# Two block orders in a Strassen kernel on Trainium2: block 2 of A11 B11 behind block 5, and k^T v one place sooner

## The chip, the cores and the metric

The kernel runs on one core of one Trainium2 chip. The metric is the device time of one execution in microseconds (us). Times of separate runs are given as a median; one further execution was taken with the hardware profiler, and everything that is said of single instructions comes from that one.

The engines of the core are named as in the profile: PE is TensorE (PEld its weight loads), DVE is VectorE, ACT is ScalarE, POOL is GpSimd and SP is SyncE, which issues most of the loads. Each engine works through its own instructions in the order in which the program issued them.

## The reference

```python
def _attn_ref(q, k, v, g_norm):                       # (8, 8, 576, 64) each
    kv = np.einsum('bhsd,bhse->bhde', k, v)
    out = np.einsum('bhsd,bhde->bhse', q, kv)
    rms = np.sqrt(np.mean(out * out, axis=-1, keepdims=True) + 1e-06)
    return (out / rms * g_norm).astype(np.float32)
...
def _moe_ref(x, w_in, w_out, s, b):                   # x: (4608, 512), d_ff = 2048
    h = x @ w_in
    r = np.maximum(h, 0.0)
    g = s * (r * r) + b
    return (g @ w_out).astype(np.float32)
```

The output of the linear attention, with its heads laid side by side, is the x of the second part. All is float32. The two large products, x by w_in and g by w_out, are nearly all of the arithmetic.

## The kernel before, in words

**Tiling.** The 4608 rows are worked in nine units of 512 rows, u = 0 to 8. "The seventh unit" is u = 6. In each unit a first stage makes g from x and w_in, and a second stage makes the output from g and w_out. While a unit runs, the attention of the next unit is made beside it, in steps that are put between the unit's own steps.

**Strassen products.** Both stages use the Winograd form of Strassen's scheme: a product of two matrices that are cut in 2 x 2 becomes seven products of blocks, numbered 1 to 7, with sums of blocks before and sums of results after. From u = 2 on, the scheme is used on two levels: each of the seven outer products of the second stage is itself made from seven inner blocks. The outer product 1 is A11 B11, where A11 is a quarter of g and B11 a quarter of w_out. Its inner blocks are what the first part of the change reorders. The other outer products are made in the groups (2, 5), (6), (7, 3) and (4).

**Inner blocks and banks.** The function `at_two_levels` returns four functions for one group. `sums` makes sums of quarters of g on VectorE (line 256 and line 253 of the profile). `go(m)` issues the matmuls of inner block m: for A11 B11 these are four matmuls of 128 x 128, which the profile records as eight. `out_of(m)` takes the result out of PSUM, and `do` calls both. The blocks 1, 6, 5 and 3 add up in one bank named x; block 2 has a bank z; the blocks 7 and 4 share a bank y. So between two blocks in x, the value that stands there has to be copied out:

- after block 1 the copy is r1 (VectorE, line 1077), wanted for the output of block 2;
- after block 6 it is r2 (VectorE, line 1077), wanted for block 4;
- after block 5 it is r4 (for A11 B11 on ScalarE, line 1077), wanted to finish the output of block 5 with y;
- after block 3 it is an output itself (ScalarE for A11 B11, line 1077).

The output adds of the blocks 2, 5 and 4 are on VectorE (line 253). The function `keep` in `at_two_levels` makes the tiles r; each tag has one buffer, and a new writer waits for the readers of the one before.

**The second stage, `rest()`.** Its order is written out by hand. At its start it still finishes blocks of the first stage (`p3_5`, `p3_34`, and `s1`, two adds on VectorE that also need two activations of ScalarE), between the inner blocks of A11 B11.

**The ring.** From u = 2 on the pieces of w_out come through a ring of 14 slots in SBUF. `ORDER` lists the pieces (outer product, inner block) in the order in which they are wanted, `pump()` issues the next loads on SP as slots come free, and `used()` says that a piece has been read. Slots come free in the order of the list alone.

**k^T v.** For u = 1 to 6, `kv_product` makes k^T v of one further batch: 144 matmuls of 64 x 64, each with a weight load, and four copies of the results (ScalarE, line 388) into `bd_kv`. Its inputs are the first eight pieces in the ring of its unit. From u = 3 on it takes the banks z and y. Where it stands is set in `sides`, in a table `first` from a place in the first stage to what is called there. In `run` of `mm1_deep`, place 2 lies between the first x1 and the second, and place 4 between the first x6 and the first y7. `A["product"]` is the attention product of the next unit's first half, 32 matmuls of 64 x 32.

Of the kernel before, what the change touches and what calls it, by code (L numbers as in the profile page):

```python
# [10 lines left out]
FP32 = mybir.dt.float32  # L11
# [6 lines left out]
def kernel(  # L18
# [40 lines left out]
    P = 128  # L59
# [192 lines left out]
    def add(o, a, b):  # L252
        nc.vector.tensor_tensor(out=o, in0=a, in1=b, op=ALU.add)  # L253
# [136 lines left out]
    late, xT = {}, {}  # L390
# [596 lines left out]

    ORDER = [(1, 1), (2, 1), (5, 1)] + [(1, m) for m in (6, 2, 7, 5, 3, 4)]  # L990
    ORDER += [(i, m) for m in (2, 6, 7, 5) for i in (2, 5)] + [(6, 1)]
    ORDER += [(i, m) for m in (3, 4) for i in (2, 5)]
    ORDER += [(6, m) for m in (2, 6, 7, 5)] + [(7, 1), (3, 1), (6, 3), (6, 4)]
    ORDER += [(i, m) for m in (2, 6, 7, 5) for i in (7, 3)] + [(4, 1), (7, 3), (3, 3), (7, 4)]
    ORDER += [(4, m) for m in (2, 6, 7, 5)] + [(3, 4), (4, 3), (4, 4)]

# [4 lines left out]
    for u in range(1, U):  # L1001
# [4 lines left out]
        else:  # L1006
            queue_w2 += [(u, key, m) for key in DEEP for m in (6, 5)]
            queue_w2 += [(u, i, m) for i, m in ORDER]
    next_at = [0]
# [44 lines left out]
    def mm2(u, step=None, side={}):  # L1054
# [43 lines left out]
        def at_two_levels(group, other, to):  # L1098

            n = len(group)
            a = {i: {} for i in group}
            t, r = {}, {}
            cols = [slice(q * P, q * P + P) for q in range(2)]

            def quarter(i, j, h):
                g = g_pair[G_OF[i], h].rearrange("p s b t -> p (s b) t")  # L1110
                return g[:, :, j * P : j * P + P]

            def sums(which, *of):
                for i in of or group:
                    x11, x12, x21, x22 = (quarter(i, j, h) for j in range(2) for h in range(2))
                    a[i].update({2: x12, 4: x22})
                    for m in which:
                        a[i][m] = late["sub"].tile(
                            [P, FC // 4, P], FP32, name="sub",
                            tag="sub7" if m == 7 else "sub", bufs=2 if m == 7 else 6,  # L1120
                        )
                        if m == 5:
                            add(a[i][5], x21, x22)
                        elif m == 6:
                            sub(a[i][6], a[i][5], x11)
                        elif m == 7:
                            sub(a[i][7], x11, x21)
                        else:
                            sub(a[i][3], x12, a[i][6])

            def go(m, *of):
                name = {2: "z", 7: "y", 4: "y"}.get(m, "x")
                first = m in (1, 2, 7)
                if first:
                    ps = bank_of((name, group), name, 1 if name == "z" else 2)
                    t[name] = ps.rearrange("p b (m c) -> p (b m) c", c=P)[:, :n]
                for i in of or group:
                    k = group.index(i)
                    x = quarter(i, 0, 0) if m == 1 else a[i][m]
                    w = ring[u, i, m]  # L1140
                    for f in range(FC // 4):
                        matmul(
                            t[name][:, k], x[:, f], w[:, f],
                            first and k == 0 and f == 0, f == FC // 4 - 1,
                        )
                    used((u, i, m))

            def keep(name, j, q):
                if name == "r2":
                    r[name] = late["tmp"].tile([P, n, P], FP32, name="r", tag=f"r2_{n}")  # L1150
                else:
                    r[name] = late["tmp"].tile([P, 2, P], FP32, name="r", tag="r14")[:, :n]
                plus_of(
                    r[name], t["x"], other(j, cols[q]),
                    nc.scalar.copy if name == "r4" else nc.vector.tensor_copy,
                )

            def out_of(m, k=slice(0, n)):
                if m == 1:
                    keep("r1", 0, 0)  # L1160
                elif m == 2:
                    add(to(0, cols[0]), t["z"], r["r1"])
                elif m == 6:
                    keep("r2", 1, 0)
                elif m == 5:
                    keep("r4", 1, 1)
                    add(to(1, cols[1]), t["y"], r["r4"])
                elif m == 3:
                    plus_of(to(0, cols[1]), t["x"], other(0, cols[1]))
                elif m == 4:  # L1170
                    add(to(1, cols[0])[:, k], t["y"][:, k], r["r2"][:, k])

            def do(*ms):
                for m in ms:
                    go(m)
                    out_of(m)

            return sums, go, out_of, do
# [139 lines left out]
        def start_5():  # L1318
# [4 lines left out]
        sums_1, go_1, out_1, do_1 = at_two_levels(  # L1323
            (1,), lambda j, q: None, one(lambda j, q: slot(j, 1)[:, q])
        )
# [28 lines left out]
        def rest():  # L1354
            do_1(1)
            start_5()
            step["p3_5"]()
            sums_1((5, 6))
            go_25(1)
            step["p3_34"]()  # L1360
            do_1(6)
            do_1(2)
            sums_1((3,))
            go_1(7)
            step["s1"]()
            do_1(5)
            sums_25((5, 6), 2)
            sums_25((7,), 5)
            at(0)
            out_25(1)  # L1370
            do_1(3)
            sums_25((5, 6), 5)
            do_1(4)
            do_25(2)
            at(1)
            step["s3"]()
            s2((0,))
            do_25(6)
            s2((1,))
            sums_25((3,))  # L1380
            go_25(7)
            s2((2,))
            do_25(5)
            s2((3,))
            sums_6(())
            do_6(1)
            sums_6((5, 6))
            at(2)
            do_25(3)
            sums_6((7, 3))  # L1390
            do_25(4)
            if end:
                for j in range(2):
                    store("o1", j, 4 * u + j, left, queues)
            s4((0,))
            do_6(2, 6)
            s4((1, 2, 3))
            go_6(7)
            do_6(5)
            sums_73((5, 6), 7)  # L1400
            sums_73((), 3)
            go_73(1)
            with_5(0, cols[0])
            out_73(1)
            do_6(3)
            with_5(0, cols[1])
            sums_73((5, 6), 3)
            do_6(4)
            with_5(1)
            do_73(2)  # L1410
            sums_73((7,))
            at(3)
            do_73(6)
            sums_73((3,))
            at("sums")
            go_73(7)
            do_73(5)
            sums_4((5, 6))
            do_4(1)
            at(4)  # L1420
            do_73(3)
            with_7(0)
            sums_4((7, 3))
            go_73(4, 7)
            out_73(4, slice(0, 1))
            with_7(1)
            if end:
                for j in range(2):
                    store("o2", j, 4 * u + 2 + j, right, queues)
                store("o1", 0, 4 * u, right, queues)  # L1430
            else:
                store("o1", 0, 4 * u, queues=queues)
            do_4(2, 6)
            go_4(7)
            do_4(5)
            at(5)
            go_73(4, 3)
            out_73(4, slice(1, 2))
            if end:
                store("o1", 1, 4 * u + 1, right, queues)  # L1440
            else:
                store("o1", 1, 4 * u + 1, queues=queues)
            do_4(3)
            at(6)
            if end:
                store("o2", 0, 4 * u + 2, left, queues)
            else:
                store("o2", 0, 4 * u + 2, queues=queues)
            do_4(4)
            if end:  # L1450
                store("o2", 1, 4 * u + 3, left, queues)
            else:
                store("o2", 1, 4 * u + 3, queues=queues)
# [63 lines left out]
    turn, take, product, square, root, norm, turn_x = zip(*(attention(c) for c in range(4)))  # L1517
# [154 lines left out]
    def sides(u, A, B):  # L1672
# [4 lines left out]
        kv = []  # L1677
# [36 lines left out]
            }  # L1714
        else:
            first = {
                2: [A["turn"]],
                4: [A["product"], *kv],
                5: [A["back"]],
                6: [A["square"], B["turn"]],  # L1720
                7: [A["row_sum"]],
# [13 lines left out]
    for u in range(U):  # L1735
        A, B = pairs_of(u + 1) if u + 1 < U else (None, None)
# [98 lines left out]
```

## Time and profile before

| | us |
|---|---|
| median of 3 runs | 911.13 |
| lowest and highest of them | 909.51, 912.71 |
| the profiled execution's own time | 908.79 |
| its span, first to last instruction | 907.0 |
| TensorE busy | 893.4 (98%) |
| VectorE busy | 659.3 (73%) |
| ScalarE busy | 347.8 (38%) |
| GpSimd busy | 266.5 (29%) |

The busy shares are averages over the whole span. A timeline row gives the start in us from the span's start, the time that the row covers in us, the engine, the line, the operation, the tiles (out<-in), the shape and the count; in square brackets stands the idle time of the engine before it, and what ended it. A line of the waits gives the waiting engine and line, what it waited for, the total in us, how often, and the longest. Ends of matmuls are modelled, so the distance from start to start is the better measure of what a block costs on TensorE.

### The profile page before, as it was taken

What the parts mean: (1) busy time and instruction counts of PE and PEld (TensorE: products, weight loads), DVE (VectorE), ACT (ScalarE), POOL (GpSimd) and SP (SyncE); (2) the same over time, 40 slices, a digit from 0 to 9 for tenths busy, and PEclk for the clock granted to TensorE, in tenths of its full rate; (3) what the DMA queues carried; (4) which work ended last, traced back from release to release, by engine and by line L of the source; (5) the groups of instructions that cost most, each with busy time, mean ns of one, the idle gap of its engine ahead of it and who ended that gap; (6) DMA issues with size and microseconds to landing.
All of it is one profiled execution on the core that took longest, in us unless ns stands there. A gap on an engine that the chain in (4) does not pass through costs nothing.

```text
span 907.0 us, 19461 instructions
## 1 busy us (share of the span) xinstructions
PE 893.4 (98%) x7578; PEld 823.0 (91%) x7578; DVE 659.3 (73%) x1240; ACT 347.8 (38%) x584; POOL 266.5 (29%) x501
## 2 busy tenths in 40 slices
PE   7999999999999999999999999999999999999998
PEld 6888888888889998999899988998899989999998
DVE  2899686687557975798578866885779667972696
ACT  3887024521157016620463037501670066104610
POOL 2027067024732434702372027403440300021000
PEclk9999999999999999999999999999999999999999
DMA  9697947259944995389537972698349811992286
GB/s 267 218 325 215 300 111 240 59 146 396 333 121 109 301 302 139 81 289 316 163 78 229 304 242 66 166 304 271 91 95 319 276 41 52 301 292 60 56 279 186
DMA packets 118987, 184.55 MB, mean 203 GB/s; under 512 B 25200, under 2 KB 42992, under 8 KB 118896
## 3 DMA queue, kind: packets, MB, share of 16 engines
q1 hardware_dynamic: 98288, 155.36, 54.5%
q0 software_dynamic: 17152, 25.72, 9.8%
q10 hardware_dynamic: 3456, 2.23, 1.0%
q8 instruction: 60, 0.98, 0.5%
q14 instruction: 31, 0.25, 0.1%
HBM read 157.03 MB, written 26.21 MB: 202 GB/s over the span
## 4 chain that ended last, share of the span: by engine, by line
PE 93%; DVE 4%; DMA 1%; ACT 1%; issue 1%; SPq 0%; DVEq 0%
PE x_ps L92 46%; PE y_ps L92 28%; PE z_ps L92 10%; PE sx_ps L92 6%; PE y_ps L540 2%; DMA kv_sb<-in_v_dram 1%; PE kv_ps L372 1%; PE z_ps L372 1%; DVE xn L573 0%; DVE a L256 0%; DVE sub L256 0%; PE y_ps L372 0%; DVE o L253 0%; DVE xT L584 0%; DVE xs L256 0%
## 5 line engine op out<-in xcount | busy, mean ns | idle before, releaser
L1610 POOL DMA_DIRECT2D q_sb<-in_q_dram x312 | 176.2, 573 | 133.0 <-ACT a L898 77.2
L92 PE MATMUL x_ps<-w_sb,sub 128*128 128x128 f32 x1176 | 149.5, 276 | 3.1 <-ACT r L1077 2.5
L1197 POOL DMA_DIRECT2D out_dram<-o x120 | 59.6, 503 | 310.2 <-issue 152.7
L92 PEld LDWEIGHTS x_ps<-w_sb,sub 128*128 128x128 f32 x1176 | 139.7, 192 | 4.8 <-ACT r L1077 3.8
L639 ACT ACTIVATE a<-a,b_col,s_col 128x512 f32<-128x512 f32 x144 | 117.0, 813 | 27.0 <-DVE a L642 18.3
L92 PE MATMUL x_ps<-xs,ws 128*128 128x256 f32 x528 | 125.2, 380 | 0.1
L92 PE MATMUL y_ps<-xs,wb 128*128 128x256 f32 x528 | 124.6, 381 | 0.0
L92 PEld LDWEIGHTS y_ps<-xs,wb 128*128 128x128 f32 x528 | 97.1, 190 | 12.4 <-issue 0.6
L92 PEld LDWEIGHTS x_ps<-xs,ws 128*128 128x128 f32 x528 | 96.3, 190 | 11.7 <-ACT r L713 0.5
L814 ACT COPY a<-x_ps 128x512 f32<-128x512 f32 x28 | 16.4, 584 | 220.4 <-PE x_ps L92 220.4
L253 DVE TENSOR_TENSOR r<-sx_ps,a 128x256 f32<-128x256 f32 x84 | 35.4, 421 | 80.3 <-PE sx_ps L92 80.3
L92 PE MATMUL x_ps<-xT,wa 128*128 128x256 f32 x360 | 83.7, 381 | 0.1
L898 ACT ACTIVATE a<-a 128x512 f32<-128x512 f32 x112 | 69.8, 623 | 18.4 <-DVE a L260 18.4
L92 PEld LDWEIGHTS x_ps<-xT,wa 128*128 128x128 f32 x360 | 66.8, 190 | 10.4 <-issue 1.5
L92 PE MATMUL x_ps<-w_sb,a 128*128 128x128 f32 (+1 forms) x432 | 64.9, 298 | 0.0
L92 PE MATMUL y_ps<-w_sb,a 128*128 128x128 f32 (+1 forms) x416 | 62.1, 295 | 0.0
L92 PEld LDWEIGHTS x_ps<-w_sb,a 128*128 128x128 f32 x432 | 58.4, 192 | 2.9 <-issue 0.4
L92 PEld LDWEIGHTS y_ps<-w_sb,a 128*128 128x128 f32 x416 | 56.1, 192 | 2.1
L253 DVE TENSOR_TENSOR r<-x_ps,o 128x256 f32<-128x256 f32 (+1 forms) x84 | 29.6, 353 | 28.8 <-PE x_ps L92 28.1
L92 PE MATMUL y_ps<-w_sb,sub 128*128 128x128 f32 x392 | 49.5, 275 | 0.0
L256 DVE TENSOR_TENSOR a<-a,a 128x512 f32<-128x512 f32 x72 | 46.8, 684 | 0.4
L92 PE MATMUL z_ps<-w_sb,a 128*128 128x128 f32 (+1 forms) x352 | 46.9, 280 | 0.0
(184 smaller groups left out, 1452.2 us busy)
## 6 DMA issues: line engine op xcount, KB each, us to landing
w_sb<-w SPq DMA_DIRECT2D x399, 256.0 KB, 4.8
w_raw<-in_moe_w_in_dram SPq DMA_DIRECT2D x8, 1024.0 KB, 6.8
w_raw<-in_moe_w_out_dram SPq DMA_DIRECT2D x8, 1024.0 KB, 5.2
w_sb<-w SPq DMA_DIRECT2D x14, 512.0 KB, 8.7
w<-sub POOLq DMA_DIRECT2D x28, 256.0 KB, 6.1
out_dram<-o POOLq DMA_DIRECT2D x112, 64.0 KB, 3.9
w_sb<-in_k_dram SPq DMA_DIRECT2D x24, 288.0 KB, 4.7
w_sb<-in_v_dram SPq DMA_DIRECT2D x24, 288.0 KB, 4.8
```

The costliest lines, as they stand in the source:

```text
L92: nc.tensor.matmul(o, lhsT=lhsT, rhs=rhs, start=start, stop=stop, skip_group_check=True)
L253: nc.vector.tensor_tensor(out=o, in0=a, in1=b, op=ALU.add)
L256: nc.vector.tensor_tensor(out=o, in0=a, in1=b, op=ALU.subtract)
L372: nc.tensor.matmul(ps[r][(r ^ l) * HB : (r ^ l) * HB + HB, i, :], lhsT=kv[l][0][rows, j, :], rhs=kv[l][1][rows, j, :], start=(j == 0), sto ...
L540: nc.tensor.matmul(ps[l][32 * p : 32 * p + 32, r, lo:hi], lhsT=bd_kv[b % 2][rows, p, at : at + 32], rhs=st["qT"][rows, p, lo:hi], start=Tr ...
L639: nc.scalar.activation(t, t, AF.Identity, scale=s_col, bias=b_col)
L814: nc.scalar.copy(g_tile("a11", s), st["x", s])
L898: nc.scalar.square(ga[name, s], ga[name, s])
L1197: queues[s % 2].dma_start(out=view[b, jj, :, cols], in_=st[name, j][s * w : s * w + w, cols])
L1610: load()
```

## The change

In every unit from u = 2 on, inner block 2 of A11 B11 is issued behind block 5 instead of behind block 6: the order 1, 6, 2, 7, 5, 3, 4 becomes 1, 6, 7, 5, 2, 3, 4. The ring's list is changed alike. Since r1 is now still wanted when r4 is written, r4 takes another buffer, of a tag (`q4`) that the first stage uses already. The new buffer applies to r4 of all groups.

In u = 6 alone, k^T v is called at place 2 of the first stage instead of place 4, behind `A["turn"]`. Its slots of the ring come free there too. Nothing is added to or taken from what is computed.

```diff
-    ORDER = [(1, 1), (2, 1), (5, 1)] + [(1, m) for m in (6, 2, 7, 5, 3, 4)]
+    ORDER = [(1, 1), (2, 1), (5, 1)] + [(1, m) for m in (6, 7, 5, 2, 3, 4)]
...
-                    r[name] = late["tmp"].tile([P, 2, P], FP32, name="r", tag="r14")[:, :n]
+                    r[name] = late["tmp"].tile(
+                        [P, 2, P], FP32, name="r", tag="r14" if name == "r1" else "q4"
+                    )[:, :n]
...
             do_1(6)
-            do_1(2)
             sums_1((3,))
             go_1(7)
             step["s1"]()
             do_1(5)
+            do_1(2)
             sums_25((5, 6), 2)
...
             first = {
-                2: [A["turn"]],
-                4: [A["product"], *kv],
+                2: [A["turn"], *(kv if u == 6 else [])],
+                4: [A["product"], *(kv if u != 6 else [])],
```

## The prediction

> **What bounds the kernel now.** I read the page's busy table and chain first, then who waited for whom on TensorE, then the timeline around the two edits.
>
> ```profile
> PE 893.4 (98%) x7578; PEld 823.0 (91%) x7578; DVE 659.3 (73%) x1240; ACT 347.8 (38%) x584; POOL 266.5 (29%) x501
> PE 93%; DVE 4%; DMA 1%; ACT 1%; issue 1%; SPq 0%; DVEq 0%
> ```
>
> TensorE is busy 98% of the span and carries 93% of the chain that ended last; its clock is at nine tenths or more in every slice. So an edit pays if it closes a hole in TensorE's stream and costs if it opens one. The holes, from the waits of TensorE (us in total, times, longest):
>
> ```profile
> PE x_ps L92 <- ACT r L1077: 2.5, 7, 0.4
> ...
> PE z_ps L372 <- issue: 0.9, 1, 0.9
> ...
> PE x_ps L92 <- DVE r L253: 0.6, 2, 0.4
> ```
>
> The first is one hole in each of the seven units u = 2 to 8. The second is in the k^T v product of u = 6. The third lies in u = 2. Around the first, in u = 6, TensorE's timeline and then ScalarE's:
>
> ```profile
> 676.25 1.06 PE L92 MATMUL x_ps<-w_sb,sub 128*128 128x128 f32 x8
> 677.14 1.06 PE L92 MATMUL z_ps<-w_sb,a 128*128 128x128 f32 x8
> 678.03 1.06 PE L92 MATMUL y_ps<-w_sb,sub 128*128 128x128 f32 x8
> 678.93 1.06 PE L92 MATMUL x_ps<-w_sb,sub 128*128 128x128 f32 x8
> 680.34 1.16 PE L92 MATMUL x_ps<-w_sb,sub 128*128 128x128 f32 x8 [0.35 <-ACT r L1077]
> 681.33 0.83 PE L92 MATMUL y_ps<-w_sb,a 128*128 128x128 f32 x6
> ```
> ```profile
> 678.49 0.81 ACT L639 ACTIVATE a<-a,b_col,s_col 128x512 f32<-128x512 f32 x1
> 680.02 0.27 ACT L1077 COPY r<-x_ps 128x128 f32<-128x128 f32 x1 [0.72 <-PE x_ps L92]
> ```
>
> These six rows are the blocks 6, 2, 7, 5, 3, 4 of A11 B11. Four of them (6, 5, 3 and the earlier 1) grow one sum in one x bank, and each value of it is copied out before the next block adds to it. Block 5 is followed at once by block 3, so block 3 waits until ScalarE has copied r4. Undisturbed blocks start 0.893 us apart; 678.93 to 681.33 is 2.40 us for two, so the hole is 2.40 - 1.79 = **0.62 us** (0.52 of waiting, and 0.10 because the first weight load no longer runs ahead). Seven times it is 4.3 us, more than the 2.5 that the wait table counts, since modelled matmul ends overlap the next start.
>
> The k^T v hole, in the chain:
>
> ```profile
> 629.83 0.91 issue
> 630.73 0.27 PE z_ps L372
> ```
>
> It is in the middle of the product, after every tensor it needs was in use, so it waits for no data. The same product in u = 5 runs from 531.41 to the next block at 533.69, 2.28 us; here from 627.63 to 631.11, 3.48 us. The hole costs **1.20 us**. The DMA view of 628 to 629 us shows what coincides:
>
> ```profile
> q8 instruction: 1, 0.02, 5.8%
> ```
>
> **What the Trainium skill says.** "Runtime: NRT & Kernel Launch", Instruction fetch mechanics: instructions stream in blocks of 16 KiB, 256 instructions, fetched by DMA as the sequencer runs, and the cost is mostly hidden because issue is slower than the refill. The trace agrees on size (queue q8: 60 packets, 0.98 MB) but not on hiding: k^T v is 288 instructions in some 2.2 us, 7.6 ns each, and directly before it u = 6 issues 64 more for the attention product. "TensorE: Matmul & The Clock Gate", Step-by-step: weight loads are pulled ahead of running matmuls; here they start 0.11 us ahead (678.82 against 678.93), and in the hole load and matmul start together, which is the 0.10 above. "Perfetto Trace Analysis", Matmuls: independent groups should rotate through different PSUM banks so that evacuation of one hides behind the next; the z block (2) is the one that can be put between two x blocks, and y is already between 2 and 5.
>
> **Part 1: block 2 moves behind block 5 (and r4 gets another buffer), u = 2 to 8.** Same instructions, other order: 6, 7, 5, 2, 3, 4.
>
> Gap 5 to 3 now holds block 2. From 6 at 676.25: 7 at 677.14, 5 at 678.03, 2 at 678.93, 3 due at 679.82. Block 5 can be read 1.09 us after its start (678.93 to 680.02 before), so at 679.12; ScalarE is in the activation that starts at 678.49, and by the spacing of its predecessors (0.72) takes the copy at 679.21 to 679.30, ending at 679.48 to 679.57; with the 0.05 from copy to TensorE, 679.53 to 679.62. Block 3's weight load is due at 679.71. It fits with 0.1 to 0.2 us: the 0.62 goes.
>
> Gap 6 to 5 loses block 2 and keeps block 7. Block 5 needs VectorE's r2 copy of block 6, in the trace 677.34 to 677.63 after 0.47 us of idle; usable at 677.68, weight load due at 677.92. Slack 0.24: no new wait, priced at nothing by VectorE's idle time.
>
> What stands behind on VectorE: the later add of block 2 (0.21) moves behind two adds "s" and the add of block 5. Working it row by row (0.60 per 512-wide operation, 0.71 where it needs the one before): r2 at 677.34, the sum for block 3 at 677.55, s at 678.15, the second s only at 679.34, as it needs ScalarE's activation that ends at 679.30, the two output adds at 679.94 and 680.15, the next sums at 680.36. Before they began at 680.53, so VectorE leads by 0.17 us while TensorE leads by 0.62. The next demands of the group (2, 5): its second sum 6 usable at 684.07, due 684.17; r2 at 686.74, due 686.86; r4 at 689.48, due 689.54. All fit, by 0.06 to 0.12; by 691 VectorE has caught up (it idles 0.31 before 689.57 and 0.56 before 695.83 today). Full value for u = 3 to 8: 6 x 0.62 = **3.7 us**.
>
> In u = 2 those demands are late already: VectorE runs without a pause from 293 to 311 us and TensorE waits for r at 300.54 and 310.14 (the third wait above). There only VectorE's lead counts: **0.2 us**.
>
> The ring order ORDER changes alike, so weights still arrive in the order of use; 7 and 5 are wanted 0.89 us sooner, by loads issued 14 slots ahead. TensorE waits for none of these loads now; cost nothing, at most one landing (longest 10.4 us against some 12 of lead). The new buffer's r4 waits only for readers of the unit's earlier q4, long done; block 1's r1 lives 1.8 us longer, and its next writer is in VectorE's own order behind it.
>
> **Part 2: k^T v before the second x1 in u = 6.** Moved: 288 TensorE instructions, four ScalarE copies of 0.26, and eight SP loads that wait for its slots (628.8 to 632 becomes some 624.5 to 628; behind them SP holds only later loads of the same ring). No POOL issue is passed. Data: the last k or v load landed at 620.07, the product would start at 622.3: 2.2 us of slack. Banks: z and y were last read by 619.9; z is next wanted at some 627, its copies done by 625.2; ScalarE is idle then (1.14 before 624.09).
>
> Instructions: what moves behind it (second x1 16, two small blocks 16, x6 16, attention product 64) is 112 instructions. Today's stop comes at about instruction 264 of the product; that boundary would then be 88 behind its end, 1.7 us of x1, 0.9 of small blocks, 1.7 of x6 and part of the attention product later, while the fetch took some 2.4 us from packet to resumption (628.35 to 630.73). So the 1.20 goes. Against it, two fast runs now lie apart: each change of form costs a restart, 0.17 in (0.09 + 0.08) where joint entry cost nothing and 0.40 out of the attention product where 0.38 stood, +0.19. Net **1.0 us**. Bounds: from +0.2 (the hole stays or reappears) to -1.3.
>
> **Sum.** 3.7 + 0.2 + 1.0 = 4.9 us. Against the profiled execution's own 908.79 us (span 907.0 and 1.8 around it) that is 903.9; that execution is 2.3 below the median 911.13, and from the median it is **906.2**.
>
> **Rivals.** (a) VectorE becomes the bound in all units as in u = 2: slacks of 0.06 to 0.12 are as small as my row arithmetic is sure. Then TensorE keeps only VectorE's 0.17 per unit: 7 x 0.17 + 1.0 = 2.2, 908.9. For: the u = 2 waits. Against: idle rows in the other units. (b) The k^T v hole is not the fetch, or turns up at another fast stretch: 3.9 - 0.2 = 3.7, 907.4. For: other fetches pass beside k^T v without a hole; against: nothing else lies in the gap. (c) The wait only changes places: block 5 waits for r2. It decides from 0.24 us of lateness; if the copy fell behind the sum and both s (1.9 us), each unit would lose 1.9 - 0.24 + 0.10 = 1.8, 12.3 in all against 5.3 gained: 918. Against: VectorE is idle ahead of that copy in every unit. (d) The edit does nothing, if order were set elsewhere: 911.1. Against: instructions go out in program order.
>
> **Chances.** Forecast 0.62, (a) 0.17, (b) 0.14, (c) 0.04, (d) 0.03. A measurement of this kernel tells 0.3%, 2.7 us, from no change. Forecast and (b) are faster, (a) lies about the line: 0.83 faster, 0.12 same, 0.05 slower. Range 904.2 to 909.2: from the forecast less 2 (the shown runs spread 3.2) to (a).
>
> **What would show it.** TensorE's wait on r L1077 gone in all seven units, blocks 0.89 apart through 6, 7, 5, 2, 3, 4; no wait of x_ps on DVE r in u = 3 to 8; the r waits of u = 2 still there and no longer offset by the first hole; k^T v of u = 6 in 2.3 us without "issue". Wrong would be: x_ps waits on DVE r at blocks 5, or an issue hole elsewhere.

## The result and the profile after

The median fell from 911.15 us to 906.44 us (lowest 905.75, highest 907.35); the ratio is 0.9947, with a 95% interval of 0.9931 to 0.9963. The forecast was 906.2.

The profiled execution after took 906.96 us, with a span of 905.2. Against the profiled execution before, the span is only 1.8 us shorter, while the medians are 4.7 apart. So the two profiles have to be laid over each other before a cause is read from them. I took TensorE's matmuls in the order of issue, both profiles having 7578 records, and followed by how much each starts later or earlier after than before:

| where | change of the distance, us |
|---|---|
| up to 73.5 us, ahead of anything that was edited | +2.92 |
| u = 2, block 3 of A11 B11 | -0.61 |
| u = 2, 7.7 us behind it, block 5 of the group (2, 5) | +0.45 |
| u = 3, 4 and 5, block 3 of A11 B11 | -0.61, -0.61, -0.62 |
| u = 4, k^T v, nothing edited there | +0.14 |
| u = 6, k^T v and its surroundings | -1.01 |
| u = 6, 7 and 8, block 3 of A11 B11 | -0.62, -0.62, -0.62 |

Without the first row the sum is -4.7 us. The row of k^T v of u = 4 was not forecast: the product took 2.42 us in place of 2.27 in this one execution, and why is not known. The first row is the start of the program, which differs from execution to execution: in the eight profiles whose start no edit touches (those of before and after, and six of the experiments) the k^T v of u = 1 begins between 151.34 and 154.27 us. The waits of TensorE after show it in two lines (waiting engine and line, releaser, us in total, times, longest), and the third wait is what is left of u = 2:

```profile
PE kv_ps L372 <- DMA kv_sb<-in_v_dram: 2.5, 4, 1.1
PE x_ps L92 <- ACT r L713: 1.7, 2, 1.1
...
PE x_ps L92 <- DVE r L253: 1.1, 2, 0.7
```

The wait on r L1077 and the "issue" wait of z_ps are not in that list any more. The two waits on line 713 end at 71.8 and 76.1 us, in the first unit, where nothing was edited; the list of before has none. From here on "from u = 1 on" is the distance from the first k^T v matmul of u = 1 to the end of the span. It leaves the start out: 907.02 - 151.34 = 755.68 us before, 905.18 - 154.27 = 750.91 after, **4.77 us less**.

The blocks of A11 B11 in u = 6, TensorE's timeline after:

```profile
676.29 1.06 PE L92 MATMUL x_ps<-w_sb,sub 128*128 128x128 f32 x8
677.18 1.06 PE L92 MATMUL y_ps<-w_sb,sub 128*128 128x128 f32 x8
678.07 1.06 PE L92 MATMUL x_ps<-w_sb,sub 128*128 128x128 f32 x8
678.97 1.06 PE L92 MATMUL z_ps<-w_sb,a 128*128 128x128 f32 x8
679.86 1.06 PE L92 MATMUL x_ps<-w_sb,sub 128*128 128x128 f32 x8
680.75 1.06 PE L92 MATMUL y_ps<-w_sb,a 128*128 128x128 f32 x8
```

Six blocks, 0.89 apart throughout; the z row now stands between the second and third x row. ScalarE's timeline for r4, and VectorE's for r2, the two adds "s" and what follows:

```profile
678.53 0.82 ACT L639 ACTIVATE a<-a,b_col,s_col 128x512 f32<-128x512 f32 x1
679.25 0.24 ACT L1077 COPY r<-x_ps 128x128 f32<-128x128 f32 x1
```
```profile
677.38 0.29 DVE L1077 COPY r<-x_ps 128x128 f32<-128x128 f32 x1 [0.47 <-PE x_ps L92]
...
679.38 0.69 DVE L253 TENSOR_TENSOR s<-a,a 128x512 f32<-128x512 f32 x1 [0.51 <-ACT a L639]
679.99 0.28 DVE L253 TENSOR_TENSOR o<-y_ps,r 128x128 f32<-128x128 f32 x1
680.19 0.28 DVE L253 TENSOR_TENSOR o<-z_ps,r 128x128 f32<-128x128 f32 x1
680.39 0.68 DVE L253 TENSOR_TENSOR sub<-a,a 128x512 f32<-128x512 f32 x1
```

r4 is copied 679.25 to 679.49 and block 3 starts at 679.86: the copy has left the path. The wait in square brackets at 679.38 is new and falls on VectorE; its next sums start at 680.39, 0.53 after block 3, where before they started 0.19 after it (680.53 against 680.34):

```profile
680.53 0.68 DVE L253 TENSOR_TENSOR sub<-a,a 128x512 f32<-128x512 f32 x1
```

That is how much nearer to the path VectorE has come.

Inside the k^T v of u = 6 no two matmuls start more than 0.09 us apart; before, one distance was 1.12. The chain of waits behind its last matmul has no "issue" piece either (start, us, what):

```profile
625.65 1.93 PE x_ps L92 x8
627.58 0.44 PE sx_ps L92 x4
628.02 0.45 PE z_ps L92 x4
628.47 1.73 PE x_ps L92 x8
630.19 1.02 PE y_ps L540 x32
```

k^T v itself takes 2.27 us (from 623.31 to the start of the next block at 625.58), and the attention product follows behind four other blocks.

### The profile page after: what moved, and what is told of

Same layout as the page of the kernel before. It is cut to its first block, busy times and chain, and to the rows that moved or that the text cites. A ratio compares the mean times of both kernels' runs of the same rounds, so it can differ in the third digit from the quotient of the medians.

```text
span 905.2 us, 19434 instructions
## 1 busy us (share of the span) xinstructions
PE 891.9 (99%) x7578; PEld 821.9 (91%) x7578; DVE 658.7 (73%) x1240; ACT 347.6 (38%) x584; POOL 266.8 (29%) x501
## 4 chain that ended last, share of the span: by engine, by line
PE 88%; DVE 6%; DMA 3%; ACT 2%; issue 1%; DVEq 0%; ACTq 0%
PE x_ps L92 43%; PE y_ps L92 25%; PE z_ps L92 10%; PE sx_ps L92 6%; PE y_ps L540 2%; DMA w_raw<-in_moe_w_in_dram 1%; DMA kv_sb<-in_v_dram 1%; DMA w_raw<-in_moe_w_out_dram 1%; PE kv_ps L372 1%; PE z_ps L372 1%; DMA q_sb<-in_q_dram 1%; DVE xs L256 1%; DVE a L256 0%; ACT w_raw L233 0%; DVE xn L573 0%
## 5 line engine op out<-in xcount | busy, mean ns | idle before, releaser
L253 DVE TENSOR_TENSOR r<-sx_ps,a 128x256 f32<-128x256 f32 x84 | 35.4, 422 | 80.1 <-PE sx_ps L92 80.1
L253 DVE TENSOR_TENSOR r<-x_ps,o 128x256 f32<-128x256 f32 (+1 forms) x84 | 29.7, 353 | 26.7 <-PE x_ps L92 26.0
```

## The experiments

**The two edits one at a time.** The first kernel is the change with the rows of k^T v put back:

```diff
-                2: [A["turn"], *(kv if u == 6 else [])],
-                4: [A["product"], *(kv if u != 6 else [])],
+                2: [A["turn"]],
+                4: [A["product"], *kv],
```

> Block 2 behind block 5 in all units, k^T v of u = 6 where it was. My theory (two separate edits that add up): no wait of TensorE on r L1077, 0.62 us saved in each of u = 3 to 8 and 0.17 in u = 2, and the hole in the k^T v of u = 6 still there with 1.1 to 1.2 us; 3.9 us less than before from u = 1 on, some 3.7 less than the median. Rival (VectorE bounds all units): 1.2 us less. Rival (the order of blocks also moved the hole): no hole, 5 us less.

Measured: 907.37 us median against 911.59 (ratio 0.9946, 0.9932 to 0.9961); from u = 1 on 751.87, which is 3.81 less than before. The waits of TensorE still have the hole of k^T v, and nothing on r L1077:

```profile
PE z_ps L372 <- issue: 0.9, 1, 0.9
```

The second kernel is the kernel before with only the move of k^T v.

> Only k^T v of u = 6 moved, blocks in the old order. My theory: the hole of 1.2 us gone, 0.2 us of restarts added, seven waits on r L1077 as before; 1.0 us less than before from u = 1 on, which the spread of whole runs can hardly show. Rival (the hole stays with the product wherever it stands): 0.2 us more.

Measured: 910.74 us median against 911.59 (ratio 0.9987, 0.9979 to 0.9996); from u = 1 on 754.73, 0.95 less. The seven waits on r L1077 are as before, and z_ps no longer waits. 3.81 + 0.95 = 4.76, and the whole change gave 4.77: the two edits add up, and both sizes are as forecast (3.9 and 1.0).

**Is it block 2, or any block?** Here block 7 is the one put between 5 and 3; no other buffer is needed, since r1 is used up before r4 is written. k^T v stays where it was.

```diff
-    ORDER = [(1, 1), (2, 1), (5, 1)] + [(1, m) for m in (6, 2, 7, 5, 3, 4)]
+    ORDER = [(1, 1), (2, 1), (5, 1)] + [(1, m) for m in (6, 2, 5, 7, 3, 4)]
...
-            go_1(7)
+            go_1(5)
             step["s1"]()
-            do_1(5)
+            go_1(7)
+            out_1(5)
```

> Blocks of A11 B11 in the order 1, 6, 2, 5, 7, 3, 4, no new buffer, k^T v where it was: block 7 and not block 2 stands between 5 and 3. My theory (any independent block hides the copy): the same gain as with block 2, 3.9 us from u = 1 on, no wait on r L1077. Rival (it matters that block 2's add comes later on VectorE, or the new buffer): the gain differs by over 1 us or the wait on r L1077 stays.

Measured: 906.85 us median (ratio 0.9942, 0.9925 to 0.9959); from u = 1 on 752.98, only 2.70 less than before, so by the letter of the expectation the number missed by over 1 us. The place-by-place comparison says why. The wait on r L1077 is gone in all seven units, and TensorE's blocks are 0.89 apart through 5, 7 and 3 (in u = 3 they start at 389.73, 390.62 and 391.51). But in u = 2, ahead of any inner block of A11 B11, TensorE waited 0.45 us for VectorE, which had stood behind a late load of q (VectorE's timeline, this kernel):

```profile
260.64 1.25 DVE L528 STREAM_TRANSPOSE qT<-q_sb 128x1024 f32<-128x1024 f32 x1 [4.98 <-DMA q_sb<-in_q_dram]
261.81 0.65 DVE L260 CUSTOM_DVE_ANT_0 a<-y_ps,a 128x512 f32<-128x512 f32 x1
```

and the hole in the k^T v of u = 6 was 1.5 us, 0.3 longer than before. Another 0.1 is in u = 2: VectorE begins the sums of the next group 0.1 later against block 3 than with block 2, and there VectorE is the bound. Each of u = 3 to 8 loses a further 0.04, some 10 us behind block 3. Without these four losses (0.45, 0.3, 0.1 and 0.2) the gain would be some 3.75, near the other order's 3.81; the first two stand in places that the edit does not touch. The medians of whole runs, which do not hang on one execution, do not show this kernel behind: 4.7 us less than before, against 4.2 with block 2, and their intervals overlap. The theory that any independent block hides the copy stands; the new buffer and the later add of block 2 are not what pays.

**Putting the hole into its other place.** The change, with block 5 directly behind block 6:

```diff
-    ORDER = [(1, 1), (2, 1), (5, 1)] + [(1, m) for m in (6, 7, 5, 2, 3, 4)]
+    ORDER = [(1, 1), (2, 1), (5, 1)] + [(1, m) for m in (6, 5, 7, 2, 3, 4)]
...
-            go_1(7)
+            go_1(5)
             step["s1"]()
-            do_1(5)
+            go_1(7)
+            out_1(5)
             do_1(2)
```

> The change, but with block 5 directly behind block 6 (1, 6, 5, 7, 2, 3, 4). My theory: the hole comes back in its other place, in front of block 5, which waits for VectorE's r2 copy, 0.5 to 0.65 us in each of seven units; 4 us more than the change. Theory of the wait that only moves: as well, but then the change itself should show part of this. Rival (VectorE's copy is early enough by itself): no hole, time of the change.

Measured: 910.48 us median (ratio to before 0.9988, 0.9982 to 0.9995); from u = 1 on 755.23, 4.32 more than the change. The waits of TensorE:

```profile
PE x_ps L92 <- DVE r L1077: 2.7, 7, 0.4
```

The same seven holes, now behind VectorE's r2 in place of ScalarE's r4, 0.55 us each and 0.10 for the first weight load, which no longer runs ahead. So the value is neither in the engine that copies nor in the number of blocks between 6 and 3, but in having at least one block in each of the two gaps, 6 to 5 and 5 to 3.

**What the hole in k^T v is.** I counted TensorE's instructions (weight loads, matmuls and its semaphore instructions) from the start. In the kernel before, the hole of u = 6 comes after 266 instructions of k^T v. Multiples of 256 counted from there fall, in u = 3 to 5, elsewhere in the product; in u = 1 and 2 they fall at 269 and 239 without a hole, and the last section comes back to that. If the hole is a wait for the next block of instructions, spare instructions at the start must move it. They were added where TensorE waits for k and v:

```diff
-    def warm(n):
+    def warm(n, more=0):
...
+        for _ in range(more):
+            matmul(ps[:HB, 0, :HB], ident[:HB, :HB], ident[:HB, :HB], True, True)
...
-                warm((18, 7)[i])
+                warm((18, 7)[i], (16, 0)[i])
```

> The change, with 64 more TensorE instructions at the start (16 spare 64 x 64 matmuls and their weight loads, the result unused), in the first microseconds where TensorE waits for k and v. My theory (the hole is the wait for a block of 256 instructions, when a block ends late in k^T v and the attention product stands right before it): the blocks then end where they did in u = 6 before, but in u = 5, so a hole of 1.1 us with no visible cause appears in the k^T v of u = 5, and none in the other units. Rival (the hole belongs to u = 6, by its data or banks): no hole anywhere.

Measured, one execution: from u = 1 on 753.62, 2.71 more than the change. The chain of waits of this kernel, in u = 5 (start, us, what):

```profile
536.70 0.05 PE z_ps L374
536.76 1.50 issue
538.26 0.21 PE z_ps L374
```

k^T v of u = 5 took 4.07 us in place of 2.28, a hole of 1.79 where the change has none, and the k^T v of no other unit has one. The place is right; the size is 1.6 times what was expected. The rest of the 2.71 is a late load of q in u = 2 (0.4), a stop of 0.2 right behind the k^T v of u = 6, and 0.5 behind the last matmul. The start of the program has a hole of this kind too, 1.0 us in the first k^T v, which "from u = 1 on" leaves out and no expectation named.

> As the one before with 128 more instructions (32 spare matmuls, which may start the rest 1 to 2 us later). My theory: block ends fall at about instruction 268 of k^T v in u = 3 and u = 4, so two holes of 1.1 us, in those two units; none in u = 5, where the end falls at 203 and the fetch has begun while slower blocks ran. Rival: no hole anywhere.

Measured, one execution: from u = 1 on 755.36, 4.45 more than the change, all of its gain but 0.3. The waits of TensorE:

```profile
PE z_ps L374 <- issue: 2.8, 3, 1.2
```

Three holes, not two: 1.51 us in u = 3 and 1.24 in u = 4, where they were expected, and 0.96 in u = 6, where none was expected. There k^T v stands at its new place, behind slower matmuls. A small one, 0.3 us of waiting, is in the first k^T v at the start. Another 0.7 came from the late load of q in u = 2 that was met above.

> The kernel before, unchanged in its orders, with 192 more TensorE instructions at the start (48 spare matmuls, 3 to 4 us later at the start). My theory: no block ends inside the late part of a k^T v, so the hole of u = 6 is gone though the product has not moved, and none appears elsewhere: 1.2 us less from u = 1 on. Rival (the place in u = 6 makes the hole): it stays.

Measured, one execution: the hole of u = 6 is gone with k^T v at its old place, every k^T v of u = 1 to 6 takes 2.27 to 2.28 us, and from u = 1 on it is 754.94, 0.74 less than before. The missing 0.4 went into a new hole right behind the k^T v of u = 2, 0.39 us, which I had not expected: the count puts the end of a block 15 instructions behind that product.

The last of this group leaves the start as it was and swaps two neighbours: the kernel before, with k^T v ahead of the attention product at place 4 of u = 6.

```diff
-                4: [A["product"], *kv],
+                4: [*kv, A["product"]] if u == 6 else [A["product"], *kv],
```

> The kernel before, but at place 4 of u = 6 alone k^T v stands ahead of the attention product and not behind it. The two block ends around it then fall at instruction 74 of k^T v and 42 instructions into the attention product, with only fast instructions between them. My theory (256 instructions pass faster than a block is fetched, whichever operation they belong to): no hole in k^T v, and one of 0.5 to 1.2 us inside the attention product. Rival (the hole belongs to the matmuls of k^T v): none in the product, 1.2 us less from u = 1 on.

Measured, one execution: from u = 1 on 755.68, the time of before. The chain of waits in u = 6:

```profile
629.91 0.98 PE y_ps L540 x20
630.89 0.54 issue
631.43 0.65 PE y_ps L540 x12
```

k^T v is whole, and the hole (0.90 us by start-to-start distances) has gone into the attention product, after 20 of its 32 matmul records, which are 40 instructions; 42 were expected. So it belongs to the count of instructions and to how fast they pass, not to k^T v, its data or its banks.

Counted over the whole program the rule is sharper than these forecasts. Number all instructions of TensorE that a trace records, from the first on. In the eleven traces of this case TensorE stood idle eleven times for over 0.15 us with no releaser that the profile shows ("issue"), and each time the first instruction behind the stop has a number that leaves 193 when it is divided by 256: 11201 in five of them (u = 6 of the kernel before, of the orders of block 2 and block 7 alone and of the kernel with 128 more, and the attention product above), 9409, 5825 and 7617 in the other moved holes, 4033 behind the k^T v of u = 2, and 449 in the two at the start.

**The waits that were left in u = 2.** The change left 1.6 us of holes there, counted from start to start. VectorE does 1.2 us of row sums for the next unit a few instructions ahead of the r2 that TensorE needs. In u = 2 alone each step of that work is called one place later:

```diff
-                0: [B["square"]], 1: [B["row_sum"], A["scale"]], 2: [B["norm"]], 3: [B["turn_x"], *q[1]],
-                "sums": [B["scale"]],
+                0: [B["square"]], 1: [A["scale"]], 2: [B["row_sum"]], 3: [B["norm"]],
+                "sums": [B["turn_x"], *q[1]], 4: [B["scale"]],
```

> The change, and in u = 2 alone the row sums, the normalisation, the transpose and the scaling of the next unit's second half are called one place later each (row sums at place 2 of the second stage, normalisation at 3, transpose at the place named sums, scaling at 4). My theory: the two waits of TensorE on r L253 in u = 2 (0.90 and 0.52 us, with restarts 1.6 in all) shrink to under 0.3 in all, since VectorE has 1.1 us less ahead of them; 1.3 us less than the change, some 6 less than before. Rival (the same VectorE work delays TensorE at its new place): waits on VectorE in u = 2 between 315 and 330 us instead, no gain.

Measured: **904.68 us** median against 911.08 (ratio 0.9934, 0.9920 to 0.9948), the best of all; from u = 1 on 749.64, 1.27 less than the change. TensorE's timeline of it, blocks 7 and 5 of the group (2, 5):

```profile
298.07 1.95 PE L92 MATMUL y_ps<-w_sb,sub 128*128 128x128 f32 x16
299.86 1.95 PE L92 MATMUL x_ps<-w_sb,sub 128*128 128x128 f32 x16
...
317.08 1.95 PE L92 MATMUL y_ps<-w_sb,sub 128*128 128x128 f32 x16
319.12 2.05 PE L92 MATMUL x_ps<-w_sb,sub 128*128 128x128 f32 x16
```

The first pair is 1.79 apart, without a hole. The change has 2.70 there:

```profile
300.60 1.95 PE L92 MATMUL y_ps<-w_sb,sub 128*128 128x128 f32 x16
303.30 2.05 PE L92 MATMUL x_ps<-w_sb,sub 128*128 128x128 f32 x16 [0.74 <-DVE r L253]
```

No wait of TensorE on r L253 is left in the list. Of the 1.27 us, 0.14 is no merit of the edit: k^T v of u = 4 takes its usual 2.27 again. The second pair above, in the group (7, 3), is 2.04 apart: about 0.25 us came back, where VectorE now does the normalisation right ahead of the value that the second of them waits for. The rival was right in kind, at a sixth of the size.

## Why the prediction was right, point by point

- **The hole between 5 and 3.** Forecast 0.62 us in each of u = 3 to 8; measured 0.61 to 0.62. The row arithmetic put r4 at 679.21 to 679.30 and VectorE's next sums at 680.36; measured, in a profile whose blocks lie 0.04 later, 679.25 and 680.39. The slack in front of block 5 was there, as VectorE idles 0.47 ahead of r2 just as before.
- **u = 2.** Forecast: only VectorE's lead of 0.17 counts. Measured -0.61 and then +0.45, together -0.16. Rival (a) is what happens in this one unit; in the others the slacks of 0.06 to 0.12 sufficed.
- **k^T v.** Forecast 1.20 saved and 0.19 of restarts; measured -1.01. That the hole is an instruction fetch was argued from one DMA packet before; the moved counts show it. The prediction's "not on hiding" is too wide, though: of the 60 packets of the kernel before, one ended in a hole.
- **The sum.** 4.9 forecast, 4.77 from u = 1 on, 4.71 between the medians. The 0.14 of the k^T v of u = 4, which no term of the forecast has, makes up the difference.
- **What was thin.** The 2.3 us between the profiled execution and the median were carried over as they stood. They are not a property of measuring: the start-up differs by 2.9 us between the two profiled executions, and that of before had the shorter one. Had the change been judged by its two spans, 1.8 us, over half of its value would have been lost to that.
- **Rival (b)** did not happen in this kernel, but its kind did with 64 or 128 instructions more. The prediction had counted where the block would end behind the moved product (88 instructions), and that held; it had counted no other unit. Since the move shifts no count outside u = 6, none was needed here, but an edit that adds or removes instructions would have needed them all.

## What to carry to other kernels

Where several blocks add up in one bank and each partial sum is copied out, look at the gaps between the members of the chain, and give every gap one independent block: here a second block in one gap was worth nothing, and a missing one cost 0.6 us per unit. A hole of TensorE without a releaser, inside a dense run of very short matmuls, may be its instructions arriving late; count instructions, and break the run up rather than tune it by chance. When an edit is worth a few us, compare the profiles place by place and leave out the start-up before reading a sum.

## What the runs showed of the hardware

TensorE's instructions came in DMA packets of 16 KiB on their own queue, 60 in a program of 15539 recorded instructions and 61 where 64 to 192 were added. In the seven holes in the k^T v of u = 3 to 6 the packet started 0.5 to 1.0 us after the first matmul of k^T v, and TensorE went on 2.3 to 2.7 us after the packet's start; 256 instructions of k^T v pass in 2.0 us. Every one of these holes was 250 to 269 instructions into it.

The same time separates all packets. Numbered as above, and with packet by packet set against the blocks of 256 in order, the next block was wanted 2.7 us or less after the start of its packet in twelve cases of all eleven traces: the eleven stops, and the one of 0.1 to 0.2 us behind the k^T v of u = 6 in the kernel with 64 more. Where 2.9 us or more lay between, TensorE did not stop. So the stops are the cases in which a packet started too shortly before its block was wanted.

The end of a block at such a place is not enough: in u = 1 and 2 of the kernel before it falls at 269 and 239, without a hole, and there the packet started 1.8 and 2.7 us ahead of k^T v. In none of the traces did a packet start more than 41 recorded instructions ahead of the end of the block before the one it brings, so never more than about one block was on its way; some started over 150 instructions behind that end. What sets this distance stays open. So does why the packet was late in u = 6 of the kernel with 128 more instructions, behind slower matmuls; the DMA engines were fully busy around that one (share 1.0 from 624 to 629 us) and about half busy around the others.
